# kv and its product with Wo on small TensorE tiles, in a transformer block with linear attention

## The chip, the cores and the metric

One core of a Trainium2 chip runs the whole program. The metric is the device time of one execution in microseconds (us), as the median of several runs, each version compared with runs of the kernel before on the same chip. One profiled execution of each version gives a trace; its span is some 1.8 us shorter than the timed run.

The engines are called PE (TensorE matmuls), PEld (its weight loads), DVE (VectorE), ACT (ScalarE), POOL (GpSimd) and SP (SyncE, which issues the transfers).

## The reference

A block with adaptive layer norm: linear attention, then a gated feed-forward part. What the change touches is the attention of 32 heads of 32 columns, over 2048 rows:

```python
kv  = jnp.einsum('bhsd,bhse->bhde', pk, v)      # one 32 x 32 matrix for each head
z   = jnp.einsum('bhsd->bhd', pk)
num = jnp.einsum('bhqd,bhde->bhqe', pq, kv)
den = jnp.einsum('bhqd,bhd->bhq', pq, z)[..., None] + 1e-06
o   = num / den
...                                             # o, heads side by side, @ wo
```

The kernel does not compute `num`. It gets kv in two steps: first G, the product of the block's input with the keys, in 16 groups of 16 matmuls, each group into one bank of PSUM (the memory that PE's results go to); ACT and DVE empty the bank, which is called an eviction, and add a row built from z (zb). Then kv is Wv times G. It multiplies kv of each head by the 32 rows of Wo that belong to the head, gets one matrix MW of 1024 x 1024, and multiplies the scaled queries by MW.

## The kernel before

Instructions are recorded first. A small class works out who has to wait for whom from the memory ranges that each instruction reads and writes, and then emits each engine's stream. A range is kept as bytes within a partition. The first term of the access pattern, which says which partitions, does not enter:

```python
def _ap_intervals(ap):
    ...
    fd = [(s, c) for (s, c) in dims[1:] if c >= 1]     # dims[0], the partitions, is left out
    ...                                                # byte ranges within a partition

# _Prog.add, for SBUF:
            for a, b in ivs:
                self.seg.access(a, b, op, is_w, deps_add)
```

The stage that matters (cuts marked; `g` in `g_group` counts 16 groups):

```python
        P.dma("wo", WO[:], wov)                          # Wo, one transfer of 2 MB
        G_BANKS = [0] + [next_bank() for _ in range(4)]  # five PSUM banks for G
        ...
        def g_group(g): ...   # PE: 16 matmuls into bank G_BANKS[g % 5]
        def g_evac(g): ...    # ACT: GTMP from ZB; DVE: G = PSUM * scale + GTMP
        def z_row():
            ...
            zw = P.dma("zw", ZDR[0].rearrange("(g p) -> g p", p=128), ZR8[0:NHG, :])
            P.wait_for("sp", [zw])
            P.dma("zr", ZB[:], ZDR[0:1, :].to_broadcast([128, D]))
        ...
        def kvt_mm(half):     # four heads at a time, 128 x 128, of which the diagonal blocks count
            for hl in range(4):
                hg = 4 * half + hl
                for dt in range(NDT):
                    P.pe("matmul", out=PS[:, 6, hl * 128:(hl + 1) * 128], lhsT=WV[:, dt, hg * 128:(hg + 1) * 128],
                         rhs=G[:, dt, hg * 128:(hg + 1) * 128], ...)
            P.dve("tensor_tensor", out=KVT[:, 4 * half:4 * half + 4, :], in0=..., in1=MASK..., op=ALU.mult)

        def m_mm(hg, banks):  # 2 matmuls of 128 x 512, then an eviction each by ACT and DVE
            ...
        for g in range(16):
            g_group(g)
            ...               # g_evac of an earlier group
            if g == 0:
                z_row()
            if g == 1:
                ...
                den()         # denominators, on 32-column tiles
            ...
```

## Time and profile before

| | before |
|---|---|
| time, median of 3 runs (range) | 832.21 us (831.06 to 833.17) |
| span of the profiled run | 829.4 us |
| PE busy | 99% |
| granted clock of PE | 1.00 |
| kv: 64 matmuls, start to start | 2 x 1.79 us |
| product with Wo: 16 matmuls | 3.45 us |

The prediction below shows the lines that carry this. A line of a timeline has the start in us, the length in us, the engine, the program's line (here always that of a helper, L176), the operation, what was written from what, the shapes and the count. Brackets at the end give the engine's idle time just before and what ended it. Matmuls overlap (a full one is 0.38 us long, and the next starts after 0.216), so their cost is read from start to start.

### The profile page before, as it was taken

The numbers are of one execution on the slowest core, as the hardware profiler recorded it, in microseconds if no ns is written. First come the engines' busy times: TensorE is split into PE (matmuls) and PEld (weight loads), VectorE is DVE, ScalarE is ACT, GpSimd is POOL, SyncE is SP. The second block draws the span as 40 slices with busy tenths as digits, with TensorE's granted clock in tenths as the row PEclk, the third lists the DMA queues.
The fourth block names the chain that finished last, engine by engine and source line by source line (L and its number), as shares of the span: only waits on it lengthen the run. The fifth ranks groups of instructions, "written<-read, shape, count | busy, mean of one in ns | idle before, by whom it ended". The sixth has DMA issues, their size and how long they took to land.

```text
span 829.4 us, 10017 instructions
## 1 busy us (share of the span) xinstructions
PE 823.2 (99%) x4083; PEld 378.8 (46%) x4083; DVE 312.6 (38%) x665; ACT 197.5 (24%) x336; POOL 39.9 (5%) x57
## 2 busy tenths in 40 slices
PE   8999999999999999999999999999999999999998
PEld 4544444444444444444444444444444444444444
DVE  5797986756955521121221112122111211221111
ACT  4757641323242111011111101111110111111011
POOL 1010000000130000030000003000000300000000
PEclk9999999999999999999999999999999999999999
DMA  9969656938397985700455571045557004553000
GB/s 321 287 151 231 148 159 171 201 104 304 60 256 229 276 264 158 192 25 15 124 155 150 153 185 33 16 124 153 154 151 190 26 18 123 154 152 87 0 26 26
DMA packets 199246, 119.28 MB, mean 144 GB/s; under 512 B 57881, under 2 KB 182945, under 8 KB 199201
## 3 DMA queue, kind: packets, MB, share of 16 engines
q1 hardware_dynamic: 199184, 118.65, 52.8%
q8 instruction: 32, 0.52, 0.3%
q14 instruction: 14, 0.11, 0.0%
q10 hardware_dynamic: 16, 0.00, 0.0%
HBM read 100.67 MB, written 4.33 MB: 127 GB/s over the span
## 4 chain that ended last, share of the span: by engine, by line
PE 97%; DMA 2%; SPq 1%; issue 0%; DVE 0%
PE ps L176 97%; DMA wsa<-in_w_mod_dram 2%; SPq L176 1%; DVE xres L176 0%
## 5 line engine op out<-in xcount | busy, mean ns | idle before, releaser
L176 PE MATMUL ps<-h2t,gug 128*128 128x512 bf16 x896 | 211.7, 379 | 0.0
L176 PE MATMUL ps<-h2t,guu 128*128 128x512 bf16 x896 | 211.7, 379 | 0.0
L176 DVE TENSOR_TENSOR at<-sg,ps 128x512 bf16<-128x512 bf16 x112 | 77.0, 687 | 282.8 <-PE ps L176 281.2
L176 ACT ACTIVATE sg<-ps 128x512 bf16<-128x512 f32 x112 | 66.9, 597 | 309.7 <-PE ps L176 309.7
L176 PEld LDWEIGHTS ps<-h2t,guu 128*128 128x128 bf16 x896 | 87.6, 98 | 105.7
L176 PEld LDWEIGHTS ps<-h2t,gug 128*128 128x128 bf16 x896 | 87.7, 98 | 105.5
L176 PE MATMUL ps<-wd_a,at 128*128 128x512 bf16 (+1 forms) x512 | 112.4, 377 | 0.0
L176 PE MATMUL ps<-ht,wqk 128*128 128x512 bf16 x512 | 111.7, 379 | 0.0
L176 PE MATMUL ps<-wd_b,at 128*128 128x512 bf16 (+1 forms) x384 | 85.0, 377 | 0.0
L176 PEld LDWEIGHTS ps<-wd_a,at 128*128 128x128 bf16 x512 | 50.1, 98 | 59.6
L176 DVE TENSOR_TENSOR ut<-att,gb_b 128x512 bf16<-128x512 bf16 (+1 forms) x32 | 14.3, 447 | 166.8 <-ACT att L176 166.8
L176 PEld LDWEIGHTS ps<-ht,wqk 128*128 128x128 bf16 x512 | 49.5, 98 | 58.7 <-DVE biasq L176 0.2
L176 ACT ACTIVATE att<-ps 128x512 bf16<-128x512 f32 (+1 forms) x32 | 17.4, 591 | 182.1 <-PE ps L176 182.1
L176 PEld LDWEIGHTS ps<-wd_b,at 128*128 128x128 bf16 x384 | 37.6, 98 | 44.7
L176 PE MATMUL ps<-pk,xres 128*128 128x512 bf16 x256 | 56.5, 379 | 0.0
L176 PE MATMUL ps<-mw,pqt 128*128 128x512 bf16 x256 | 56.3, 379 | 0.0
L176 POOL TENSOR_SCALAR h2t<-h2t,modcol 128x512 bf16<-128x512 bf16 x32 | 26.3, 836 | 383.4 <-DMA h2t<-xn 383.4
L176 ACT ACTIVATE e<-ps 128x512 bf16<-128x512 f32 x56 | 33.1, 603 | 31.7 <-PE ps L176 19.8
L176 PEld LDWEIGHTS ps<-mw,pqt 128*128 128x128 bf16 x256 | 24.9, 98 | 30.2 <-DVE xres L176 0.4
L176 PEld LDWEIGHTS ps<-pk,xres 128*128 128x128 bf16 x256 | 24.9, 98 | 29.9 <-issue 0.4
L176 ACT ACTIVATE junk<-xres 128x1024 bf16<-128x1024 bf16 x24 | 25.4, 1058 | 35.1 <-DVE xres L176 34.9
L176 DVE SCALAR_TENSOR_TENSOR xres<-ps,xres 128x512 bf16<-128x512 f32 x32 | 21.4, 688 | 12.3 <-PE ps L176 11.5
(107 smaller groups left out, 344.8 us busy)
## 6 DMA issues: line engine op xcount, KB each, us to landing
gug<-in_B_w_gate_dram SPq DMA_DIRECT2D x56, 512.0 KB, 4.0
guu<-in_B_w_up_dram SPq DMA_DIRECT2D x56, 512.0 KB, 5.3
xres<-in_A_x_dram SPq DMA_DIRECT2D x20, 256.0 KB, 7.7
rb<-recip_den SPq DMA_DIRECT2D x8, 512.0 KB, 11.5
stgx<-in_w_mod_dram SPq DMA_DIRECT2D x2, 2048.0 KB, 7.9
wd_a<-in_B_w_down_dram SPq DMA_DIRECT2D x4, 1024.0 KB, 7.8
out_dram<-xres SPq DMA_DIRECT2D x31, 128.0 KB, 1.7
xres<-in_A_x_dram SPq DMA_DIRECT2D x3, 1024.0 KB, 14.1
```

The source lines that it names most:

```text
L176: return getattr(e, method)(**kw)
```

## The change

The intent: a head's kv is 32 x 32, but the kernel before computes 128 x 128 for four heads and masks 12 of 16 blocks away. PE can work as smaller tiles side by side, as it already does for the denominators (32 matmuls on 32-column tiles in 1.84 us, where 32 full ones at 0.216 would take 6.9). So kv is computed head by head on 32-column tiles and kept compact, and the product with Wo runs on 32 by 32 tiles, 16 of them at a time. For that, the changed kernel puts the rows of Wo that one row of tiles reads into one quarter of the partitions, so Wo is loaded in another order, in eight pieces of 32 partitions.

```diff
-        wov = A_wo.rearrange("(kt p) n -> p kt n", p=128)
+        wov = A_wo.rearrange("(f g h e) n -> f g e h n", f=2, g=4, h=4)
...
-        P.dma("wo", WO[:], wov)
+        for f in range(2):
+            for g in range(4):
+                P.dma("wo%d%d" % (f, g), WO[32 * g:32 * g + 32, 4 * f:4 * f + 4, :], wov[f, g])
...
         def kvt_mm(half):
+            for h in range(4):
                 for dt in range(NDT):
+                    for g in range(4):
+                        c0 = 512 * half + 128 * g + 32 * h
+                        P.pe("matmul", out=PS[32 * g:32 * g + 32, 6, 32 * h:32 * h + 32], lhsT=WV[:, dt, c0:c0 + 32],
+                             rhs=G[:, dt, c0:c0 + 32], ...)
+            P.dve("tensor_copy", out=KVT[:, half, :], in_=PS[:, 6, 0:128])
+
+        def m_mm(half, nh, banks):
+            for k in range(4):
+                for g in range(4):
+                    h = (g + k) % 4
+                    P.pe("matmul", out=PS[32 * h:32 * h + 32, banks[g], :],
+                         lhsT=KVT[32 * g:32 * g + 32, half, 32 * h:32 * h + 32],
+                         rhs=WO[32 * g:32 * g + 32, 4 * half + h, nh * 512:(nh + 1) * 512], start=True, stop=True, ...)
+            ...               # four evictions, by ACT and DVE in turn
```

Cut: the old bodies, one G group's bank, and the order of the first output blocks behind the second half.

More of the change, by code (lines that the diff above doesn't have):

```diff
@@ L353, in bass_adaLN_cond__linear_attn_block__swiglu_ffn__prompt_kernel @@
         ZR8 = T("zr8", 205 * KB + 512, [128, 128], FP32)
-        KVT = T("kvt", 188 * KB, [128, NHG, 128], BF16)
+        KVT = T("kvt", 188 * KB, [128, 2, 128], BF16)
         ZSEL = T("zsel", SM + 7168, [128, 288], BF16)
@@ L904, in g_group @@
             h, dt = g // NDT, g % NDT
-            bank = G_BANKS[g % 5]
+            bank = G_BANKS[1 if g == 14 else g % 5]
             for st in range(NST):
@@ L911, in g_evac @@
             h, dt = g // NDT, g % NDT
-            bank = G_BANKS[g % 5]
+            bank = G_BANKS[1 if g == 14 else g % 5]
             i = g % 2
@@ L952, in kvt_mm @@
         def kvt_mm(half):
-            for hl in range(4):
-                hg = 4 * half + hl
+            for h in range(4):
                 for dt in range(NDT):
-                    P.pe("matmul", out=PS[:, 6, hl * 128:(hl + 1) * 128], lhsT=WV[:, dt, hg * 128:(hg + 1) * 128],
-                         rhs=G[:, dt, hg * 128:(hg + 1) * 128], start=(hl == 0 and dt == 0), stop=(dt == NDT - 1),
-                         skip_group_check=True)
-            P.dve("tensor_tensor", out=KVT[:, 4 * half:4 * half + 4, :],
-                  in0=PS[:, 6, :].rearrange("p (g d) -> p g d", g=4),
-                  in1=MASK[:].unsqueeze(1).to_broadcast([128, 4, 128]), op=ALU.mult)
@@ L963, in bass_adaLN_cond__linear_attn_block__swiglu_ffn__prompt_kernel @@
-        m_ctr = [0]
-        def m_mm(hg, banks):
-            for nh in range(2):
-                i = m_ctr[0]
-                m_ctr[0] += 1
-                bank = banks[i % len(banks)]
-                P.pe("matmul", out=PS[:, bank, :], lhsT=KVT[:, hg, :], rhs=WO[:, hg, nh * 512:(nh + 1) * 512],
-                     start=True, stop=True)
-                dst = MW[:, hg, nh * 512:(nh + 1) * 512]
-                if i % 2 == 0:
-                    P.act("activation", out=dst, in_=PS[:, bank, :], func=ACT.Copy)
+                    for g in range(4):
+                        c0 = 512 * half + 128 * g + 32 * h
+                        P.pe("matmul", out=PS[32 * g:32 * g + 32, 6, 32 * h:32 * h + 32], lhsT=WV[:, dt, c0:c0 + 32],
+                             rhs=G[:, dt, c0:c0 + 32], start=(h == 0 and dt == 0), stop=(dt == NDT - 1),
+                             skip_group_check=True)
@@ new lines, in kvt_mm @@
+            P.dve("tensor_copy", out=KVT[:, half, :], in_=PS[:, 6, 0:128])
[5 more added lines that the diff above has]
+                         lhsT=KVT[32 * g:32 * g + 32, half, 32 * h:32 * h + 32],
+                         rhs=WO[32 * g:32 * g + 32, 4 * half + h, nh * 512:(nh + 1) * 512], start=True, stop=True,
+                         skip_group_check=True)
+            for g in range(4):
+                dst = MW[:, 4 * half + g, nh * 512:(nh + 1) * 512]
+                if g % 2 == 0:
+                    P.act("activation", out=dst, in_=PS[:, banks[g], :], func=ACT.Copy)
@@ L975, in m_mm @@
                 else:
-                    P.dve("tensor_copy", out=dst, in_=PS[:, bank, :])
+                    P.dve("tensor_copy", out=dst, in_=PS[:, banks[g], :])
         def fold_ga(jt):
@@ L1011, in bass_adaLN_cond__linear_attn_block__swiglu_ffn__prompt_kernel @@
                 kvt_mm(0)
-            if 11 <= g < 15:
-                m_mm(g - 11, [MB, 7])
+            if 11 <= g < 13:
+                m_mm(0, g - 11, [MB, 7, G_BANKS[4], 6])
             if 7 <= g < 15:
@@ L1025, in bass_adaLN_cond__linear_attn_block__swiglu_ffn__prompt_kernel @@
         wo_part(0, 1, range(2, 4))
-        wo_part(1, 0, range(3))
-        m_mm(4, [4, 5, 7, 6])
-        wo_part(1, 0, (3,))
-        wo_part(1, 1, (0,))
-        m_mm(5, [4, 5, 7, 6])
-        wo_part(1, 1, range(1, 3))
-        m_mm(6, [4, 5, 7, 6])
-        wo_part(1, 1, (3,))
-        m_mm(7, [4, 5, 7, 6])
+        wo_part(1, 0, range(1))
+        m_mm(1, 0, [4, 5, 7, 6])
+        wo_part(1, 0, range(1, 4))
+        wo_part(1, 1, range(4))
+        m_mm(1, 1, [4, 5, 7, 6])
         for ch in range(1, NCH):
@@ L1076, in bass_adaLN_cond__linear_attn_block__swiglu_ffn__prompt_kernel @@
         for st in range(NST):
-            for nh in range(2):
-                wo_part(st, nh, range(4, 8) if st < 2 else range(8))
-                wo_res(st, nh)
+            for (sw, nh) in (((0, 0), (1, 0)), ((0, 1), (1, 1)))[st] if st < 2 else ((st, 0), (st, 1)):
+                wo_part(sw, nh, range(4, 8) if st < 2 else range(8))
+                wo_res(sw, nh)
             if st >= 1:
```

## The prediction

> **What bounds the kernel now.** I read the page first (busy shares, chain), then the order of work on TensorE where kv and its product with Wo are made, then what releases the first groups of that stage, then the transfer rates there.
>
> ```profile
> PE 823.2 (99%) x4083; PEld 378.8 (46%) x4083; DVE 312.6 (38%) x665; ACT 197.5 (24%) x336; POOL 39.9 (5%) x57
> ...
> PE 97%; DMA 2%; SPq 1%; issue 0%; DVE 0%
> ```
>
> TensorE (PE) is busy 99% of 829.4 us and is 97% of the chain that ended last. After the first 21 us it hardly waits, so the time is the sum of what its instructions occupy: a change pays only what it takes out of, or puts into, that stream. The timeline of PE, columns start us, length, engine, what:
>
> ```profile
> 166.72 1.95 PE L176 MATMUL ps<-g,wv 128*128 128x128 bf16 x32
> 168.51 3.62 PE L176 MATMUL ps<-pk,xres 128*128 128x512 bf16 x16
> 171.96 0.59 PE L176 MATMUL ps<-wo,kvt 128*128 128x512 bf16 x2
> 172.40 0.38 PE L176 MATMUL ps<-pk,xres 128*128 128x512 bf16 x1
> ```
>
> The length holds the pipeline's tail, so I read cost from start to start. One half of kv (32 matmuls of 128 columns) takes 168.51 - 166.72 = 1.79 us, 56 ns each; two matmuls of the product with Wo take 172.40 - 171.96 = 0.44 us, 216 ns each (a long run, such as 16 from 168.51 to 171.96, gives the same 216). So the changed work is small: 2 x 1.79 + 16 x 0.216 = 7.0 us of 832, 0.85%. Even if it vanished the kernel would not be 2% faster.
>
> The kernel already has one block with 32-column tiles, the denominators (weights 128*32):
>
> ```profile
> 130.24 3.62 PE L176 MATMUL ps<-pk,xres 128*128 128x512 bf16 x16
> 133.79 1.91 PE L176 MATMUL ps<-pqt,zsel 128*32 128x512 bf16 x32
> 135.63 0.60 PE L176 MATMUL ps<-pk,xres 128*128 128x512 bf16 x2
> ```
>
> Thirty-two tiled matmuls take 135.63 - 133.79 = 1.84 us, where 32 full ones would take 6.9: four column tiles do run together (8 rounds x 0.216 = 1.73). The surplus 0.11 is the change of mode on the way out; on the way in, the 16 before should end at 130.24 + 16 x 0.216 = 133.70, and the block starts at 133.79, so 0.1 more. I take **0.2 us per tiled block**.
>
> The second place that matters is who lets the G groups go:
>
> ```profile
> 144.12 1.33 ACT L176 ACTIVATE gtmp<-zb,modcol 128x512 f32<-128x512 f32 x2 [16.09 <-DMA zb<-z_row]
> 144.87 1.41 DVE L176 SCALAR_TENSOR_TENSOR g<-ps,modcol,gtmp 128x512 bf16<-128x512 f32 x2 [3.28 <-ACT gtmp L176]
> ...
> 131.35 1.29 SPq L176 DMA_DIRECT2D wo<-in_A_wo_dram  x1
> 132.68 0.53 SPq L176 DMA_DIRECT2D z_row<-zr  x1
> 140.08 0.33 SPq L176 DMA_DIRECT2D zb<-z_row  x1
> ```
>
> The brackets give the idle time before and its releaser. The tiny z_row write is issued at 132.68 behind Wo in the same queue; the read of zb, which needs it landed, only goes out at 140.08, and ACT waits for zb until 144.12. The first eviction of a G group then ends at 144.87 + 0.75 = 145.62 us. There are five G banks, so the sixth group waits for this eviction. It starts at 135.63 + 3 x 3.453 = 145.99: **a slack of only 0.37 us**, and the Wo load stands ahead of it.
>
> [...]32 one-column matmuls from 25.30 to 26.11 us, 25.3 ns each; but the block of denominators shows that it does not bind between different column tiles. [...]rb, which is loaded in 32-partition pieces in the very order that the change gives Wo:
>
> ```profile
> 133.40:140.00 6.60, 6.60 (x56) 2.78 (x54) 5.61 (x6) 0.00 (x0) 0.00 (x0) 1.00 0.91 318
> 150.00:155.00 5.00, 5.00 (x25) 2.25 (x23) 3.50 (x6) 1.45 (x2) 0.00 (x0) 1.00 1.02 212
> ```
>
> These are stretches, the last number being GB/s: Wo in one piece over 128 partitions runs at 318, rb at 212 with the engines fully busy.
>
> **Part by part.**
>
> *kv.* 64 matmuls of 128*128 x 128 become 256 of 128*32 x 32: a quarter of the columns, but four times the instructions, 256 in each half with the weight loads. Array work: 32 rounds of four tiles at 25.3 ns is 0.81 us, plus 0.2 for the mode, against 1.79: that would save 0.8 us a half. But 256 instructions must get in. [...]3.5 us a half, **+1.7 a half, +3.4 us in all**, all on PE's stream.
>
> *The product with Wo.* 16 full matmuls (3.45 us) become 64 of 32*32 x 512 in four blocks of 16, each block covering all 16 tiles once. If all 16 run together a block is one pass of 0.216 + 0.2 for the modes plus some 0.1 of issue: 0.52 us, four are 2.1: **-1.3 us**. If only four run together a block is 0.86 + 0.2, and the sum is +0.8 instead.
>
> *Evictions.* Sixteen of mw remain, now four after each block. In the second half the second block wants the banks of the first: two evictions of 0.69 us on VectorE and two of 0.60 on ScalarE plus 0.2 of latency are 1.6 us, and seven matmuls (1.51 us) stand between: a wait of 0.1. The kvt eviction shrinks (128 columns for 512) and stays covered by three matmuls (0.65 us). The mask multiply cost PE nothing.
>
> *Wo load.* One transfer becomes eight, each into 32 partitions, the first four to partitions 0-31, 32-63, 64-95, 96-127.[...] 2.10 MB at 318 GB/s are 6.6 us, at 213 they are 9.85: z_row behind it lands 3.2 us later, so do zb and the first eviction, and PE stalls before the sixth G group by 3.2 - 0.37 = **+2.9 us**. Later groups have their slack back (the second eviction follows after 0.67 us, its group 3.45 us after). Eight issues at the 0.43 us of rb's make 3.5 us on the queue instead of 1.3; with transfers of 256 KB at 213 GB/s (1.2 us each) the issue does not bind.
>
> Sum: 832.2 + 3.4 - 1.3 + 0.1 + 2.9 = **837.3; I say 837**.
>
> **Rivals.** (a) *The array bounds kv, not the issue*: -0.8 a half. For it: bursts within the denominators' block; against it: that block is 64 instructions[...]. Then 832.2 - 1.6 - 1.3 + 0.1 + 2.9 = 832.3, and without the stall 829.4. [...](c) *No stall*: the 32-partition pieces do not slow the load, because rb also re-reads one small row buffer and that might be its limit. Then 834.4.[...] (d) *The clock drops*[...]: the granted clock is 1.00 in every stretch I read, also around a block of one-column matmuls (0.8 us)[...]. It would add 2 to 4 us. (e) *A gain* by over 2% would need 16 us; only 7 are there.
>
> **Range and chances.** I give (a) 25%[...]; the stall 75%. Corners: 829.4 (a, no stall)[...]. The range that should hold it 8 times in 10 is 831 to 843.5. Two per cent is 16.6 us, out of reach of every sum but the worst with a dropped clock: slower 3%, faster 1%, within 2% 96%.
>
> **What would show it.** On PE's timeline of the changed kernel: the start-to-start length of each 128-matmul kv block (3.5 us right; 1.0 means the array bounds it[...]); each 16-matmul block (0.5 against 1.06); an idle time before the sixth G group released by DVE's g, with ACT's wait for zb ending near 147.4 instead of 144.12 us; the rate while Wo lands (about 215 GB/s). The prediction is wrong if kv comes in under 1.79 us a half, if PE does not wait for g, or if the granted clock falls below 1.00 near 146 or 170 us.

## The result, and the profile after

| | before | changed |
|---|---|---|
| time, median of 4 runs | 831.74 us | 844.66 us |
| range | 831.06 to 833.17 | 844.50 to 845.06 |
| span of the profiled run | 829.4 us | 842.9 us |
| mean granted clock | 1.000 | 0.992 |

The ratio is 1.0154 (95% interval 1.0136 to 1.0171). Here and below a ratio is the mean time of one kernel's fast runs over that of the other's in the same job, so it is not quite the ratio of the medians. The changed kernel is 12.9 us slower; I had said 4.8 us.

PE's waits in the changed kernel, longest first (total us, times, longest):

```profile
PE ps L176 <- DVE g L176: 12.9, 1, 12.9
PE ps L176 <- DMA cs<-in_c_dram: 2.2, 1, 2.2
PE ps L176 <- issue: 2.0, 6, 1.1
```

One wait holds nearly the whole loss, and it is the one that I had named: the sixth G group waits for the first eviction of a G group. Only it is four times as long as I said. The timeline around it, SP first:

```profile
130.94 20.00 SPq L176 DMA_DIRECT2D wo<-in_A_wo_dram  x8
150.99 0.33 SPq L176 DMA_DIRECT2D z_row<-zr  x1
153.53 0.36 SPq L176 DMA_DIRECT2D zb<-z_row  x1
157.14 1.33 ACT L176 ACTIVATE gtmp<-zb,modcol 128x512 f32<-128x512 f32 x2 [29.45 <-DMA zb<-z_row]
157.90 1.41 DVE L176 SCALAR_TENSOR_TENSOR g<-ps,modcol,gtmp 128x512 bf16<-128x512 f32 x2 [16.98 <-ACT gtmp L176]
158.70 1.03 PE L176 MATMUL ps<-pk,xres 128*128 128x512 bf16 x2 [12.87 <-DVE g L176]
```

Against the lines of before: Wo's issue took 1.29 us and z_row went out at 132.68 us. Now the eight issues stretch over 20.00 us and z_row goes out at 150.99. From there the chain is as before: zb, ACT's gtmp, DVE's g, PE. The landing rate in this stretch is no hint of a busy path. The next answer covers stretches of the same trace; its columns after the times are the busy time of PE, PEld, DVE, ACT and POOL (count), then the granted clock, the busy share of the transfer engines, and GB/s:

```profile
145.90:149.50 3.60, 0.00 (x0) 0.00 (x0) 0.00 (x0) 0.00 (x0) 0.00 (x0) 1.00 0.41 127
149.60:158.60 9.00, 0.00 (x0) 0.00 (x0) 0.70 (x2) 1.33 (x2) 0.00 (x0) 0.50 0.31 106
158.70:163.20 4.50, 4.28 (x10) 1.65 (x12) 2.77 (x4) 3.48 (x5) 0.00 (x0) 0.50 0.95 227
163.30:167.80 4.50, 4.50 (x22) 2.06 (x21) 1.95 (x3) 0.72 (x1) 0.00 (x0) 1.00 1.03 213
```

Two things are to be seen. While Wo trickles in, the transfer engines are busy 30 to 40%: the pieces are not slow, they are not there. And the idle time costs twice: the clock falls to one half during it, and after PE has work again it stays there to 163.2 us, so that in 4.5 us PE starts 12 weight loads instead of 21.

The tiled blocks, from PE's timeline of the changed kernel:

```profile
181.74 1.26 PE L176 MATMUL ps<-g,wv 128*32 128x32 bf16 x128
...
186.49 0.43 PE L176 MATMUL ps<-wo,kvt 32*32 32x512 bf16 x16
186.86 3.63 PE L176 MATMUL ps<-pk,xres 128*128 128x512 bf16 x16
...
206.40 0.43 PE L176 MATMUL ps<-wo,kvt 32*32 32x512 bf16 x16
206.77 1.04 PE L176 MATMUL ps<-mw,pqt 128*128 128x512 bf16 x4
208.93 11.38 PE L176 MATMUL ps<-mw,pqt 128*128 128x512 bf16 x51 [1.13 <-issue]
```

A block of 16 takes 186.86 - 186.49 = 0.37 us, with the 0.09 on the way in 0.46. For kv the first full matmul after the block lacks its record; its weight load starts at 182.93, so the block takes 1.19, with the way in 1.28 us. Both are gains. The last line shows a pause of 1.13 us that ends with nothing in the profile ("issue"); neither the kernel before nor my prediction had it.

The sum for the profiled runs, 13.5 us apart: the idle time, start to start and less one matmul's 0.216, 13.0; eleven matmuls at 0.427 instead of 0.216, +2.3; kv 2 x (1.28 - 1.79) = -1.0; the product with Wo 4 x 0.46 - 3.45 = -1.6; the pause +1.3 from start to start. That is 14.0, and the stage began 0.3 us earlier in this run: 13.7.

### The profile page after: what moved, and what is told of

It is laid out like the page before. It is cut to its first block, busy times and chain, and to the rows that moved or that the text cites. A ratio compares the mean times of both kernels' runs of the same rounds, so it can differ in the third digit from the quotient of the medians.

```text
span 842.9 us, 10429 instructions
## 1 busy us (share of the span) xinstructions
PE 818.1 (97%) x4244; PEld 376.7 (45%) x4323; DVE 311.9 (37%) x665; ACT 197.3 (23%) x336; POOL 39.7 (5%) x57
## 4 chain that ended last, share of the span: by engine, by line
PE 89%; DVE 5%; DMA 5%; issue 1%; ACT 0%; SPq 0%; DVEq 0%; ACTq 0%
PE ps L176 89%; DMA wo<-in_A_wo_dram 2%; DVE acc L176 2%; DMA stg<-in_w_mod_dram 1%; DVE pkt L176 1%; DVE e L176 1%; DMA xres<-in_A_x_dram 0%; DVE pqt L176 0%; DVE mhl L176 0%; DMA zb<-z_row 0%; DMA z_row<-zr 0%; SPq L176 0%; DVE stats L176 0%; ACT xres L176 0%; DVE g L176 0%
## 5 line engine op out<-in xcount | busy, mean ns | idle before, releaser
L176 PE MATMUL ps<-pk,xres 128*128 128x512 bf16 x250 | 57.6, 389 | 13.7 <-DVE g L176 12.9
L176 DVE SCALAR_TENSOR_TENSOR xres<-ps,xres 128x512 bf16<-128x512 f32 x32 | 21.5, 688 | 13.0 <-PE ps L176 12.9
## 6 DMA issues: line engine op xcount, KB each, us to landing
xres<-in_A_x_dram SPq DMA_DIRECT2D x3, 1024.0 KB, 13.7
```

Of the source, the lines that this page charges most:

```text
L176: return getattr(e, method)(**kw)
```

## The experiments

Ten kernels ran, all with the right result. Why do eight issues take 20 us? The program as built answers for its own part. This is the list of SP's transfers in the changed kernel, with what each waits for:

```
wo<-in_A_wo_dram 32x4x1024
wo<-in_A_wo_dram 32x4x1024 [waits lane_wo00]
wo<-in_A_wo_dram 32x4x1024 [waits lane_wo01]
wo<-in_A_wo_dram 32x4x1024 [waits lane_wo02]
wo<-in_A_wo_dram 32x4x1024 [waits pe]
wo<-in_A_wo_dram 32x4x1024 [waits lane_wo10]
wo<-in_A_wo_dram 32x4x1024 [waits lane_wo11]
wo<-in_A_wo_dram 32x4x1024 [waits lane_wo12]
z_row<-zr_104 8x128 [waits dve]
```

The four pieces of each half go to different partitions but to the same bytes within a partition, and the bookkeeping knows bytes alone. So it takes each piece for an overwrite of the one before and waits for its landing (a median of 2.9 us from issue to landing in this run, 2.8 to 4.0). (`lane_wo00` is the semaphore that the landing of that piece raises.) The trace agrees: the second piece goes out at 134.92 us, 0.01 us after the first has landed. Theory A: this chain of false waits is the loss. Rivals: landing 32 partitions at a time is slow whatever waits; or the tiles cost the time.

### The eight pieces without waits (e1), and the load alone in the kernel before (e2, e3)

For e1 the changed kernel issues its eight pieces as one recorded operation, so none waits for another. That is free of races, since no two pieces touch the same bytes of the same partition.

```diff
-                P.dma("wo%d%d" % (f, g), WO[32 * g:32 * g + 32, 4 * f:4 * f + 4, :], wov[f, g])
+            outs = [WO[32 * g:32 * g + 32, 4 * f:4 * f + 4, :] for f in range(2) for g in range(4)]
+            ins = [wov[f, g] for f in range(2) for g in range(4)]
+            def fn(e):
+                return [e.dma_start(out=o_, in_=i_) for o_, i_ in zip(outs, ins)]
+            P.add("sp", fn, reads=[], writes=outs, lane="wo", ninc=8, tag="wo")
```

> The changed kernel with its eight Wo transfers issued as one operation, so that none waits for another; the order of all else is kept. Theory A (the pieces wait for each other because the kernel's own bookkeeping takes pieces of different partitions for one place): TensorE's idle time on DVE's g falls from 12.9 us to what the half-rate landing alone makes, 2.5 to 3.5 us, and the clock does not fall to half for 13 us; time 832 to 835 us. Rival B (landing 32 partitions at a time is slow by itself, whatever waits): the idle time stays near 13 us and the time at 844. Rival C (pieces without waits land as fast as one transfer): no idle time, 829.5 to 831.5.

Runs e2 and e3 take the kernel before, with all its arithmetic, and cut only its Wo load into eight pieces: e2 with a recorded transfer for each, hence with the chain, e3 as one operation.

```diff
-        P.dma("wo", WO[:], wov)
+        P.dma("wo%d%d" % (f, g), WO[32 * g:32 * g + 32, 4 * f:4 * f + 4, :],      # e2
+              wov[32 * g:32 * g + 32, 4 * f:4 * f + 4, :])
```

> The kernel before with nothing changed but its Wo load, cut into the same eight pieces with the same waits. Theory A: the load alone carries the whole loss and hides the gain of the tiles, so this is slower than the changed kernel: 831.7 + 12.9 of idle time + 2.3 of half clock = 847 (845.5 to 848.5). Rival (the small tiles cost the time): 831 to 834.

> The kernel before with its Wo load cut into eight pieces that do not wait for each other. If landing 32 partitions at a time runs at half rate (about 213 GB/s, as rb does), zb comes 3 us later and TensorE waits 2.5 to 3.5 us on DVE's g: 834.5 to 836. If the pieces run at the full rate: 831.5 to 832.5.

| run | median us (before beside it 831.21) | ratio (95%) | PE's wait for DVE's g |
|---|---|---|---|
| e1, tiles, no chain | 835.08 | 1.0051 (1.0036 to 1.0066) | 2.6 us |
| e2, no tiles, chain | 847.99 | 1.0200 (1.0185 to 1.0215) | 14.7 us |
| e3, no tiles, no chain | 835.21 | 1.0054 (1.0038 to 1.0071) | 2.6 us |

Each lies in the range of theory A, except that e1 is a hair over its own. PE's wait in e1 and in e2:

```profile
PE ps L176 <- DVE g L176: 2.6, 1, 2.6
PE ps L176 <- DVE g L176: 14.7, 1, 14.7
```

e2 shows that the load alone, without the new tiles, makes the kernel slower than the whole change did; the tiles are cleared. e1 shows that the chain is the cause. PE's line after the wait in e3:

```profile
148.59 1.68 PE L176 MATMUL ps<-pk,xres 128*128 128x512 bf16 x6 [2.58 <-DVE g L176]
```

What is left without the chain is the landing of my prediction, which the expectations call half-rate (rb's 212 GB/s, about half of the 397 that the kernel before moves from 190 to 195 us): 2.58 us idle, 2.96 - 0.216 = 2.74 us lost from start to start; I had said 2.9. The rate in e3 from 133.4 to 143 us was 216 GB/s, with the transfer engines busy 98% of it. And e3 shows a second cost: in two of its four runs the mean clock was 1.000 (833.78 and 834.37 us), in the other two 0.998 (836.05 and 836.64). Only the first of the four left a trace, so where the clock fell in the slower two is not seen. The trace of e1 shows it, in the run of 836.68 us: behind this wait, and again behind a later pause of 2.02 us, the clock was at half for 3.4 us, in which 8 or 9 matmuls start where some 16 would at 0.216, so it costs half of that, 1.7 us, each time. (The columns are those of the table of stretches above.)

```profile
148.70:152.10 3.40, 3.18 (x8) 1.22 (x8) 2.58 (x4) 2.82 (x5) 0.00 (x0) 0.50 0.81 236
199.90:203.30 3.40, 3.18 (x9) 1.21 (x8) 1.40 (x4) 0.52 (x1) 0.00 (x0) 0.50 1.07 390
```

### Wo out of the way (e4)

The pieces as one operation again, issued after z_row is written and zb's read is issued:

```diff
             if g == 0:
                 z_row()
+                wo_load()
```

> The changed kernel with Wo's eight pieces as one operation that is issued after z_row is written and zb's read is issued, so Wo stands in nobody's way. Theory A: no idle time on DVE's g at all, clock at full; what is left is the gain of the tiles alone: 0.5 us a half for kv and 1.6 us for the product with Wo, 2.6 us, less the pause of about 1.3 us that the changed kernel shows near 207.6 us if that stays: 829 to 831. If the tiles cost time: over 832.

830.64 us against 831.21, ratio 0.9992 (0.9977 to 1.0007), a difference within the noise. The wait for g is gone and the clock is at 1.000. Both kinds of tile keep their gain, yet only 0.6 us of the 2.6 us arrive. The rest is in one place of PE's timeline:

```profile
187.78 1.19 PE L176 MATMUL ps<-g,wv 128*32 128x32 bf16 x128
189.13 0.59 PE L176 MATMUL ps<-mw,pqt 128*128 128x512 bf16 x2 [0.16 <-issue]
189.66 0.43 PE L176 MATMUL ps<-wo,kvt 32*32 32x512 bf16 x16
190.02 1.68 PE L176 MATMUL ps<-mw,pqt 128*128 128x512 bf16 x7
191.64 0.44 PE L176 MATMUL ps<-wo,kvt 32*32 32x512 bf16 x16
192.00 1.04 PE L176 MATMUL ps<-mw,pqt 128*128 128x512 bf16 x4
195.02 2.32 PE L176 MATMUL ps<-mw,pqt 128*128 128x512 bf16 x9 [1.98 <-issue]
```

The pause of the changed kernel is there again and longer, 1.98 us idle (2.1 from start to start, less one matmul). The built program has no wait at its place: the pause comes after the fourth of eight full matmuls that wait for nothing; only the ninth has a wait. I counted what PE's records hold up to the pause (weight loads twice, since all of them are recorded, plus semaphore instructions): 2754 in the changed kernel, in e1 and in e4, though the pause comes at 207.4, 196.7 and 192.7 us.

### What the pause is: shifts of PE's stream (e5, e6, e9, e10, control e8)

Theory F: PE waits for its own instructions. Transfers of the kind "instruction" are listed in the page, 32 of 16 KB in the kernel before, 34 in the changed one. PE's 4083 matmuls and 4083 weight loads in the kernel before are 8166 instructions, 255 for each of the 32. A kv block now uses 256 instructions in 1.2 us; before, 256 lasted about 27 us (128 full matmuls at 0.216). Rival G: some eviction or transfer at that place in the work. The two part when instructions are added far ahead: F moves the pause, G leaves it. So, on top of e4, small matmuls take the place of warm-up matmuls at the start:

```diff
-        warm(13, bank=3)
+        warm(7, bank=3)
+        tiny(63)             # 64-column matmuls on the same operands
...
-        warm(5, bank=3)
+        tiny(44)             # together 96 matmuls, 192 instructions more
```

> The kernel with Wo after z_row, in which TensorE pauses about 2.1 us after its recorded instruction 2754 (in three kernels with different timing, always the same count). Here 96 small matmuls (with weight loads 192 instructions) more stand in place of warm-up matmuls at the start, where TensorE has little to do. Theory F (the pause is a wait for the next 16 KB of instructions, 256 of them, because the kv block uses up 256 in 1.1 us): the edge of the block of 256 moves 192 instructions earlier in the work, to where it is passed at leisure; the pause after the second product with Wo vanishes or stays under 0.5 us, and the time falls to 828 to 829.5. Rival G (the pause is a wait for an eviction or a transfer at that place in the work): it stays where it is in the work, near 2.1 us, and the time at 830.6.

> As the run with 192 instructions more, but with 128. Theory F: the edge now falls into the second kv block, right after the edge before it was passed, so the pause moves into that block (32x32 matmuls of kv) and gets longer, 3 to 6 us; time 831.5 to 835. Rival G: the pause stays after the second product with Wo, 2.1 us, time 830.6.

> Control: the kernel before with the same 192 instructions more at the start. It has no such pause, so its time should not change: 831 to 832, or up to 0.5 us more if the small matmuls delay the first transposes.

| run | median us (before 831.53) | ratio (95%) | pause in PE's timeline |
|---|---|---|---|
| e5, e4 + 192 instructions | 828.71 | 0.9966 (0.9954 to 0.9979) | none over 0.2 us |
| e6, e4 + 128 instructions | 828.97 | 0.9973 (0.9961 to 0.9986) | none over 0.2 us in this stage |
| e8, before + 192 instructions | 832.78 | 1.0019 (1.0005 to 1.0032) | none in this stage |

e5 came as F said; e6 did not. Its pause should have moved into the second kv block and grown, and it vanished. That rejects G as well, for the work was the same, but it showed that I did not know when a block is asked for. With 128 more, the block comes long before it is wanted: in e6's trace the 10th transfer of instructions, the one that is needed after count 2754, runs at 180.28 us, and that count is reached at 188.88. The control e8 missed too: it is 1.25 us slower than the kernel before, where at most 0.5 was allowed. Its trace has an extra 0.6 us before a group of one-column matmuls near 16 us, idle for the transfer of their weights (wca), and 0.9 us near 229.5, idle for an eviction by DVE. So the shift itself is not free in the kernel before, and it does not flatter e5.

So I refined F, by an estimate of mine of when a block is asked for that no trace had shown: an edge of a block just behind the start of a kv block should be worst. Shifts of 32 and 64 instructions put it there.

> The kernel with Wo after z_row and 32 instructions more at the start. Refined theory F: [...]the block is at hand some 7 us later (187.9 to 195.0 us in the kernel without shift). The edge moves 32 instructions earlier in the work, still right behind the start of the second kv block: the pause comes after the same recorded count, 2754, but 32 instructions earlier in the work, inside or before the second product block of the second half, and is longer, 2.5 to 3.3 us; time 830.5 to 832.5. Rival G (the pause belongs to a place in the work, and the shifts by 128 and 192 removed it by another way): it stays after the second product block, 2.1 us.

> As the last, with 64 instructions more. Refined theory F: [...]the next one is at hand near 191.7 and is wanted near 190: a pause of 0 to 1.7 us, before or inside the first product block of the second half; time 828.7 to 830.5. Rival G: the pause stays after the second product block, 2.1 us.

| run | median us (before 831.26) | ratio (95%) | pauses: from the last start before to the first after, after recorded count |
|---|---|---|---|
| e9, e4 + 32 | 832.70 | 1.0016 (0.9999 to 1.0032) | 1.46 us after 2242; 2.29 us after 2754 |
| e10, e4 + 64 | 835.52 | 1.0044 (1.0021 to 1.0066) | 2.88 us after 2242; 2.33 us after 2754 |

PE's timeline of e9, where the pause now cuts the second product block in two after its fourth matmul, and of e10, where one comes in the G group behind the first kv block:

```profile
193.06 0.40 PE L176 MATMUL ps<-wo,kvt 32*32 32x512 bf16 x4
195.36 0.43 PE L176 MATMUL ps<-wo,kvt 32*32 32x512 bf16 x12 [1.91 <-issue]
```

```profile
166.94 1.32 PE L176 MATMUL ps<-g,wv 128*32 128x32 bf16 x128
168.19 1.04 PE L176 MATMUL ps<-pk,xres 128*128 128x512 bf16 x4
171.73 1.55 PE L176 MATMUL ps<-pk,xres 128*128 128x512 bf16 x6 [2.50 <-issue]
```

The pause keeps its count and changes its work, and a second one appears 512 counts earlier; in the next table that is two transfers of instructions earlier, so 256 counts for each. That fits a fetch of blocks of 256, and no eviction. The packets of the 16 KB transfers (queue q8) in the kept traces show the fetches themselves:

| run | pause after count | transfer of instructions, from to us | PE goes on at |
|---|---|---|---|
| changed | 2754 | the 10th, 206.46 to 207.51 | 208.93 |
| e1 | 2754 | the 10th, 196.54 to 197.58 | 199.14 |
| e4 | 2754 | the 10th, 192.41 to 193.46 | 195.02 |
| e9 | 2242 | the 8th, 170.51 to 171.72 | 173.16 |
| e9 | 2754 | the 10th, 192.90 to 193.94 | 195.36 |
| e10 | 2242 | the 8th, 168.94 to 170.31 | 171.73 |
| e10 | 2754 | the 10th, 193.79 to 194.89 | 196.27 |

The same count always waits for the same transfer, and PE goes on 1.4 to 1.6 us after its end. What makes a fetch start, and what fills the 1.4 us after it, stays open. A rush of other transfers is not needed: during the first pauses of e9 and e10 51 and 54 GB/s were moving, during the other five 380 to 388.

My sizes were off: e9's pause did not reach 2.5 us and its time is 0.2 us above its range, and e10 has two long ones where I expected one of up to 1.7, and is 5 us above its range. The clock explains the rest of e10: behind each of its pauses in the profiled run it fell to half for 3.4 us, and the mean of its four runs lies between 0.996 and 1.000. In the profiled run of e9 it fell behind the second pause. The line of e9, then that of the second fall in e10:

```profile
195.80:199.20 3.40, 3.40 (x9) 1.22 (x10) 1.99 (x4) 1.09 (x2) 0.00 (x0) 0.50 1.05 387
196.80:200.30 3.50, 3.50 (x24) 1.00 (x23) 1.25 (x3) 1.04 (x3) 0.00 (x0) 0.51 1.06 388
```

What sets 1.91 us idle (e9), after which it falls, apart from 2.58 (e3), after which it does not, can be read from the traces, though no run was made for it: in the changed kernel, e1, e9 and e10 every time between two changes of the clock during the program's work is a whole multiple of 3.413 us (in the changed kernel 143.36 and 13.65, in e1 143.36, 3.41, 47.79, 3.41). On that grid, counted in each trace from its first change to full clock, each of the five idle times after which the clock fell (e1 2.61 and 2.02, e9 1.91, e10 2.50 and 1.94) has at least 1.91 us inside one step, and the fall comes at the end of that step; the two that did it no harm are cut by an edge (e3 1.77 + 0.81, e4 0.78 + 1.20).

### The order over the tiles (e7)

On top of e5, the kv matmuls go eight times to one column tile before the next:

```diff
-                for dt in range(NDT):
-                    for g in range(4):
+                for g in range(4):
+                    for dt in range(NDT):
```

> As the run with 192 instructions more, but the kv matmuls go eight times to one column tile before the next, instead of in turn to the four. If the order over the tiles is what makes kv fast (theory: successive matmuls on one tile start 25 ns apart, as the one-column matmuls do, on four tiles together), each kv block takes 128 x 25 ns = 3.2 us instead of 1.2, and the time is about 4 us more, 832 to 833.5. If only the rate of issue counts (8 ns for a matmul with its weight load), it stays at 828 to 829.5.

830.44 us, ratio 0.9987 (0.9973 to 1.0001): 1.7 us more than e5, from another run of the same job. Its two kv blocks in PE's timeline:

```profile
166.70 2.16 PE L176 MATMUL ps<-g,wv 128*32 128x32 bf16 x128
...
188.40 2.16 PE L176 MATMUL ps<-g,wv 128*32 128x32 bf16 x128
```

2.16 us against the 1.2 of the rotating order, in each half; the length holds the last matmul's tail of 0.18, so a matmul comes every 15.5 ns. So the order over the tiles is worth 0.95 us a half, but the 25 ns that I expected for one tile is not its floor: both expectations missed, one on each side.

## Why the prediction was wrong

**What bounds the kernel, and where it would be lost**: right. PE's stream set the time, the gain of the tiles could not pass 7 us, and the place of the loss was the sixth G group waiting behind Wo, z_row and zb, with the slack of 0.37 us worked out from the timeline.

**The Wo load, the step that failed**: "with transfers of 256 KB at 213 GB/s (1.2 us each) the issue does not bind". I took the eight pieces as free of each other. They wait for one another, because the bookkeeping leaves out partitions. The model for the estimate, rb, could not show this: its transfers are recorded four at a time as one operation, so none of the four waits for another. The term of +2.9 us measured 13.0. Without the chain it measured 2.74 (e3), so the slower landing (216 GB/s there, 318 for the one transfer) was right, and rival (c), no stall, is refuted.

**The clock, rival (d)**: "It would add 2 to 4 us". That was an estimate of mine, with no trace behind it. It added 2.3, so the size was right; I had left it out of the sum. With a stall of 2.6 us it comes in some runs and not in others: the mean clock of e3 is 1.000 in two runs and 0.998 in two.

**kv**: the term of +3.4 us measured -1.0. The 3.5 us a half in it were an estimate of mine that no trace showed: with 1.19 us for 128 matmuls and 128 weight loads, an instruction takes 4.6 ns. Rival (a), the array, gave -1.6 and was nearer. The hint for it was in the trace before: in the denominators' block four matmuls on different tiles start within 0.01 us (133.79 to 133.80).

**The product with Wo**: -1.3 was said, -1.6 measured; all 16 tiles do run together (0.37 us a block), and the 16 start within 0.05 us, where I had put 0.1 for the issue.

**Evictions**: no wait of PE for an eviction of mw shows in the changed kernel's waits; the 0.1 us said for it cannot be told from nothing.

**The pause**: in no step at all. I asked how fast instructions can be issued, and not how fast they come from memory.

The whole of it: the sum had two wrong terms of opposite sign (the load 10.1 us too small, kv 4.4 too large) and two that were not in it (clock 2.3, pause 1.3). So the error in kv hid part of the error in the load, by luck. Mended, the tiles are a gain: e5 takes 828.71 us, 0.34% less than the kernel before. It carries the tiles, Wo behind z_row, and a shift of the instruction stream that a later edit of the program would undo. Wo behind z_row was not run without the tiles; that the gain is theirs is read from the lengths of their blocks.

## What to carry to other kernels

When one transfer is cut into several, look at the waits of the program as built before reasoning about bandwidth: bookkeeping that knows less than you do (bytes but not partitions) can turn independent pieces into a chain, and whatever stands behind them in the same queue pays. Many small matmuls on several tiles can be very cheap (9.3 ns each with its weight load here), but count the instructions as well as their time: a burst that uses up a few hundred in a microsecond (256 in 1.2 us here) can run PE dry of instructions (idle for 1.1 to 2.5 us here), at a place that moves with every edit. And the cost of an idle PE does not end with the idle time, since the clock may come back late: here pauses of 1.9 us sufficed to halve it for 3.4 us.
